# Attention into two gated layers on one core: loads held 16 units back, other transfer prices in the plan, words scaled on GpSimd

## The chip, the cores and the metric

The kernel runs on one core of one Trainium2 chip. The metric is the device time of one execution in microseconds (us); lower is better. TensorE (PE) multiplies matrices, VectorE (DVE), ScalarE (ACT) and GpSimd (POOL) do element work, and SyncE (SP) issues nearly all transfers, in the order of its own queue.

## What is computed

```python
def _attn_ref(q, k, v, g_q, g_k):        # q, k, v: (4, 12, 448, 64)
    ...
    q_n, k_n = (rmsnorm(q, g_q), rmsnorm(k, g_k))
    scale = 1.0 / np.sqrt(q.shape[-1])
    scores = scale * np.matmul(q_n, k_n.transpose(0, 1, 3, 2))
    ...                                  # softmax over the last axis gives attn
    return np.matmul(attn, v).astype(np.float32)

def _moe_ref(x, w_in, w_out):            # w_in (768, 2048), w_out (2048, 768)
    h = x @ w_in
    relu6 = np.clip(h + 3.0, 0.0, 6.0)
    g = h * relu6 / 6.0
    return (g @ w_out).astype(np.float32)

def _moe2_ref(x, w_in, w_out):
    h = x @ w_in
    r = np.maximum(h, 0.0)
    g = r * r
    return (g @ w_out).astype(np.float32)

    # reference: x is the attention output as (1792, 768)
    x = _moe_ref(x=x, **moe_kwargs)
    return _moe2_ref(x=x, **moe2_kwargs)
```

Attention comes first, for 4 batches of 12 heads; its result passes through two layers, each a product into 2048 columns, a gate, and a product back to 768.

## The kernel before, in words

**Numbers in two halves.** Products run in f16. Each float32 operand is split into a high and a low f16 half, and three of the four products of halves are added. The weights arrive as 64-bit words, and `convert` makes them into halves, one unit at a time: `load` (DMA into a tile `wr`), `sign` on DVE into a tile `wf`, `dx` (a multiplication of the high words by 2^-112, on ACT or DVE), `d1` (a byte of the low words, on ACT), `join` on DVE, a maximum, a scale for the family of units, and the split into `ws` (`hi` and `lo`). The halves are used at once and stored (`spill`); later units with the same weights load them from there (`again`).

**Units.** `UNITS` lists 272 units of products in the order in which PE does them: for each layer m and batch b, 16 "in" units (18 products each) and 18 "out" units (18 or 15 products), the last 6 of them behind the next batch's "in" units. There are 4608 products in all (L1014), each 128x128 by 128x448. Batch b of the first layer needs the attention of batch b: its "in" units begin at product 0, 480, 1056 and 1632. Units 0 to 27 and 44 to 49 convert the first layer's weights, units 130 to 163 and 180 to 185 the second layer's.

**Attention.** A step (b, p) takes two heads. `norms` loads q and k (`qk`), squares and sums them, takes the inverse root on GpSimd (L448 to L453), scales, splits, and transposes by DMA into `T` (L513); two more transfers make `W`, with the halves swapped. PE makes scores (`ps_s`, L696), DVE the row maximum, ACT the exponential. In the 11 steps named in `ACROSS`, PE transposes the exponentials (L666) and multiplies in float32 (L773). In the other 13 the probabilities are split (`p`) and transposed by DMA into `pt` (L741), and PE multiplies there (`ps_a`, L792).

**What sets the order.** `Plan.order` is a list scheduler that runs when the program is built. Each task has a key, the engines on which it can run with a guessed time, tasks it depends on, and buffers. `STEPS`, `SCALE` and `VMAX` give the keys of attention's tasks in units of the products; `LOOK` and `LOOK0` say how many units ahead weights are loaded and converted. A transfer (`xfer`) is put one behind the other on a single line. The scheduler only writes down the order of each engine and which engine does a task that may run on two; on the chip every engine takes its list in order and waits where data or a buffer is missing.

Of the kernel before, what the change touches and what calls it, by code (L numbers as in the profile page):

```python
# [37 lines left out]
def units():  # L38
# [19 lines left out]
STEPS = (  # L58
    (-85.2638, -84.5299, -76.4585, -66.4326, -62.0971, -61.7424),
    (-14.9266, -4.9125, 0.9188, 14.2707, 1.5272, 9.9697),  # L60
    (28.6516, 33.3075, 36.1555, 43.5753, 49.5311, 53.688),
    (67.1629, 67.9195, 73.2971, 102.3362, 73.5949, 89.3515),
)
SCALE = (0.4278, 0.4, 0.6456, 0.4916)
VMAX = (-67.3424, 17.8405, 50.7595, 55)

SHORT = {1, 2}
LOOK = (4.0538, 5.2083)
LOOK0 = (8.2895, 6.1085, 2.0783)
GROUP = (1, 2, 2, 2)  # L70
# [34 lines left out]
class Plan:  # L105
# [168 lines left out]
def tile_kernel(ctx: ExitStack, tc: tile.TileContext, qk, v, vn, g, ident, w1i, w1o, w2i, w2o, out):  # L274
    nc = tc.nc
# [112 lines left out]
    def norms(j, p, k0, sc):  # L388
# [127 lines left out]
        if fast:  # L516
# [30 lines left out]
            t_l1 = task(km + .04, [("DVE", dve2(448), lambda: los(1))], [t_h1], [vq, vsrc])  # L547
            t_t0 = task(km + .1, [("SP", 600, lambda: trs(0))], [t_l0], [vsrc, vT], xfer=800)
            t_w = task(km + .12, [("SP", 600, tr_rev)], [t_lr, t_hr], [vrev, vW], xfer=800)
            t_tr = task(km + .11, [("SP", 600, lambda: trs(1))], [t_l1], [vsrc, vT], xfer=800)  # L550
            t_trs = [t_t0, t_tr]
            first.append(t_w)
        else:
# [3 lines left out]
            t_lo = task(k0 - 14.7 * sc, [("DVE", dve2(896), lo)], [t_hi], [vq, vsrc])  # L557
            t_trs = [task(k0 - 14.6 * sc, [("SP", 1200, tr)], [t_lo], [vsrc, vT], xfer=1570)]
        prep[b, p] = vT, t_trs, vW, t_w


    def attention(j, p, k0, sc):
# [157 lines left out]
        for r in range(0 if across else NT):  # L720
# [16 lines left out]
            for x in rows[r]:  # L737

                def ptr(r=r, vp=vp, x=x):
                    h, a, z, at, col = x  # L740
                    nc.sync.dma_start_transpose(  # L741
                        out=tl(vpt[h], [P, NV, n], F16)[:, :, col:col + z - a],
                        in_=tl(vp)[at:at + z - a, r % 2].rearrange("p a t -> p (a t)"),
                    )

                t_pt[x[0]].append(task(kk + 2.2 * sc, [("SP", 650, ptr)], [t_pl], [vp, vpt[x[0]]], xfer=(x[2] - x[1]) * 6))

# [118 lines left out]
    def convert(m, i0, ns):  # L866
# [5 lines left out]
        for x, (i, n) in enumerate(zip(ids, ns)):  # L872
# [117 lines left out]
    def unit(b, m, i, n):  # L990
# [17 lines left out]
        for a, z in cuts:  # L1008
# [257 lines left out]
```

## Time and profile before

| | |
|---|---|
| median of 3 runs | 1203.03 us (1201.07 to 1203.38) |
| the profiled execution | 1209.35 us, of which the profile's span is 1207.6 us |
| TensorE | 1123.3 us busy, 93% of the span, mean granted clock 0.977 |
| VectorE | 719.0 us, 60% |
| ScalarE | 703.9 us, 58% |
| GpSimd | 104.2 us, 9% |
| DMA | 231.18 MB moved, mean 191 GB/s |

Shares are means over the whole span. Up to about 607 us attention, conversion and products run side by side; behind that there are products, gates and the second layer's conversion alone. The mean granted clock is in parts of the full TensorE clock of 2.4 GHz; its other level is half of it.

### The profile page before, as it was taken

The numbers are of one execution on the slowest core, as the hardware profiler recorded it, in microseconds if no ns is written. First come the engines' busy times: TensorE is split into PE (matmuls) and PEld (weight loads), VectorE is DVE, ScalarE is ACT, GpSimd is POOL, SyncE is SP. The second block draws the span as 40 slices with busy tenths as digits, with TensorE's granted clock in tenths as the row PEclk, the third lists the DMA queues.
The fourth block names the chain that finished last, engine by engine and source line by source line (L and its number), as shares of the span: only waits on it lengthen the run. The fifth ranks groups of instructions, "written<-read, shape, count | busy, mean of one in ns | idle before, by whom it ended". The sixth has DMA issues, their size and how long they took to land.

```text
span 1207.6 us, 17036 instructions
## 1 busy us (share of the span) xinstructions
PE 1123.3 (93%) x6070; PEld 583.7 (48%) x6070; DVE 719.0 (60%) x1653; ACT 703.9 (58%) x1375; POOL 104.2 (9%) x142
## 2 busy tenths in 40 slices
PE   1889999799899989989999999999999999999998
PEld 0455555355444444434445545454455555555554
DVE  6989999989799967887813527878126000200300
ACT  2889899998778767755711417977356033213400
POOL 3511211101111211120000000000000000000000
PEclk9989999799999989998999999999999999999999
DMA  9755567679999899998643366869736444453351
GB/s 251 216 166 156 187 200 251 200 180 304 224 282 272 220 220 259 211 205 175 168 125 118 109 197 213 289 209 317 284 101 204 160 141 130 124 168 103 105 159 54
DMA packets 214743, 231.18 MB, mean 191 GB/s; under 512 B 137873, under 2 KB 174865, under 8 KB 214657
## 3 DMA queue, kind: packets, MB, share of 16 engines
q1 hardware_dynamic: 214592, 229.95, 66.6%
q8 instruction: 48, 0.79, 0.3%
q14 instruction: 39, 0.31, 0.1%
q0 software_dynamic: 64, 0.13, 0.1%
HBM read 156.47 MB, written 36.18 MB: 160 GB/s over the span
## 4 chain that ended last, share of the span: by engine, by line
PE 61%; DVE 14%; DMA 12%; ACT 9%; issue 2%; SPq 1%; POOL 1%; ACTq 0%; DVEq 0%
PE m L1014 49%; PE ps_s L696 3%; PE ps_a L792 3%; PE ps_s L666 2%; PE ps_a L773 2%; DVE nm L703 2%; DMA pt_0B<-p 2%; DMA qk<-in_qk_dram 1%; DMA wr<-in_w2o_dram 1%; ACT wf L898 1%; PE ps_r L759 1%; DMA ws<-spill 1%; ACT wr L889 1%; DVE p L733 1%; DVE ws L942 1%
## 5 line engine op out<-in xcount | busy, mean ns | idle before, releaser
L1014 PEld LDWEIGHTS <-ws 128*128 128x128 f16 x4608 | 446.1, 98 | 427.7 <-issue 18.5
L1014 PE MATMUL m<-g,ws 128*128 128x448 f16 x2304 | 459.5, 354 | 5.2 <-DVE g L1111 2.6
L1014 PE MATMUL m<-x,ws 128*128 128x448 f16 x1152 | 234.8, 353 | 1.3 <-DMA ws<-spill 0.9
L1014 PE MATMUL m<-yk,ws 128*128 128x448 f16 x1152 | 221.4, 353 | 0.6 <-DMA ws<-spill 0.6
L656 ACT ACTIVATE e<-ps_s,nm,esc 128x448 f32<-128x448 f32 x168 | 121.8, 726 | 22.4 <-DVE nm L713 22.0
L703 DVE TENSOR_REDUCE nm<-ps_s 128x1 f32<-128x448 f32 x168 | 102.6, 615 | 9.7 <-PE ps_s L696 9.3
L1045 ACT ACTIVATE t<-m,inv 128x448 f32<-128x448 f32 x64 | 39.5, 622 | 99.2 <-PE m L1014 99.1
L1194 ACT ACTIVATE o<-m,ov 128x448 f32<-128x448 f32 x24 | 14.5, 630 | 137.1 <-PE m L1014 137.1
L1043 ACT ACTIVATE t<-m,half,six 128x448 f32<-128x448 f32 x64 | 46.0, 721 | 58.9 <-PE m L1014 58.8
L901 DVE TENSOR_SCALAR wf<-wr 128x768 int32<-128x768 int32 (+1 forms) x68 | 35.8, 531 | 55.9 <-PE m L1014 50.5
L898 ACT ACTIVATE wf<-wr 128x768 uint8<-128x768 uint32 (+1 forms) x68 | 68.6, 1014 | 0.0
L696 PE MATMUL ps_s<-T,W 128*128 128x448 f16 (+1 forms) x192 | 63.0, 373 | 5.4 <-DMA W<-W_0r 2.8
L905 DVE SCALAR_TENSOR_TENSOR wf<-wr,wf 128x768 int32<-128x768 int32 (+1 forms) x68 | 61.4, 905 | 9.8 <-ACT wf L898 9.4
L942 DVE SCALAR_TENSOR_TENSOR ws<-wf,w_s,ws 128x768 f16<-128x768 f32 (+1 forms) x68 | 65.1, 963 | 3.1 <-ACT ws L935 2.5
L696 PE MATMUL ps_s<-T 128*128 128x448 f16 (+1 forms) x192 | 63.7, 379 | 0.2 <-DVE xr L779 0.2
L666 PE MATMUL ps_s<-eye,e 128*112 128x128 f32 x308 | 51.2, 302 | 12.1 <-ACT e L656 11.9
L1049 DVE SCALAR_TENSOR_TENSOR gr<-t,m 128x448 f32<-128x448 f32 x64 | 39.4, 616 | 38.7 <-ACT t L1043 38.3
L1052 DVE SCALAR_TENSOR_TENSOR gr<-t 128x448 f32<-128x448 f32 x8 | 5.0, 621 | 94.7 <-ACT t L1045 94.6
L733 DVE SCALAR_TENSOR_TENSOR p<-e,su,p 128x448 f16<-128x448 f32 x91 | 59.7, 678 | 1.8 <-ACT p L727 1.3
L889 ACT ACTIVATE wr<-wr 128x768 f32<-128x768 f32 (+1 forms) x60 | 52.2, 870 | 13.7 <-DVE wf L901 13.7
L337 DVE TENSOR_REDUCE g_s<-gm 128x1 f32<-128x16 f32 x4 | 0.7, 164 | 95.8 <-ACT gr L1055 95.6
L727 ACT ACTIVATE p<-e,su 128x448 f16<-128x448 f32 x78 | 49.4, 659 | 10.0 <-DVE su L642 4.7
(202 smaller groups left out, 1305.8 us busy)
## 6 DMA issues: line engine op xcount, KB each, us to landing
ws<-spill SPq DMA_DIRECT2D x132, 384.0 KB, 3.5
ws<-spill SPq DMA_DIRECT2D x72, 320.0 KB, 3.5
spill<-ws SPq DMA_DIRECT2D x44, 384.0 KB, 4.0
wr<-in_w1i_dram SPq DMA_DIRECT2D x16, 768.0 KB, 5.3
wr<-in_w2i_dram SPq DMA_DIRECT2D x16, 768.0 KB, 6.0
qk<-in_qk_dram SPq DMA_DIRECT2D x23, 448.0 KB, 4.7
wr<-in_w1o_dram SPq DMA_DIRECT2D x12, 640.0 KB, 4.9
spill<-ws SPq DMA_DIRECT2D x24, 320.0 KB, 4.8
```

The lines of the kernel that those rows point to most:

```text
L656: nc.scalar.activation(tl(ve)[:, r % 2], tl(vps)[:, 0:S], AF.Exp, bias=sums["nm"][:, r:r + 1], scale=esc, accum_out=sums["su"][:, r:r + 1])
L666: nc.tensor.transpose(o[:, c], tl(ve)[:, r % 2, c * VR:(c + 1) * VR], eye)
L696: nc.tensor.matmul(ps[at:at + z - a, 0:S], q_[:, a:z], ks[:, h * S:(h + 1) * S], start=(i == 0), stop=(i == 1))
L703: nc.vector.tensor_reduce(sums["nm"][:, r:r + 1], tl(vps)[:, 0:S], axis=AX.X, op=ALU.max, negate=True)
L727: nc.scalar.activation(tl(vp)[:, r % 2, 0], tl(ve)[:, r % 2], AF.Copy, scale=sums["su"][:, r:r + 1])
L733: nc.vector.scalar_tensor_tensor(tl(vp)[:, r % 2, 1], tl(ve)[:, r % 2], sums["su"][:, r:r + 1], tl(vp)[:, r % 2, 0], op0=ALU.mult, op1=ALU ...
L889: nc.scalar.activation(x_, x_, AF.Copy, scale=2.0 ** -112)
L898: nc.scalar.activation(low, l_.bitcast(U32), AF.Copy, scale=2.0 ** -29 * (1 - 2.0 ** -9), bias=-0.49)
L905: nc.vector.scalar_tensor_tensor(w, words()[1], 3, w, op0=ALU.logical_shift_left, op1=ALU.bitwise_or)
L942: nc.vector.scalar_tensor_tensor(tl(vws)[:, 1, 0:nf].rearrange("p k c -> p (k c)"), tl(vwf)[:, 0:nw], up, hi, op0=ALU.mult, op1=ALU.subtract)
L1014: nc.tensor.matmul(tl(vph)[:, 0:S], w[:, wa, k], tl(rhs[k])[:, xa], start=(first_ and k == 0 and c == 0), stop=(last and k == nf - 1 and c ...
L1043: nc.scalar.activation(tl(vt), tl(vph)[:, 0:S], AF.Relu, bias=half, scale=six[:, row:row + 1])
```

## The change

Five kinds of edit, all in the tables and tasks of the plan, and one new way to run a task.

1. `STEPS`, `SCALE`, `VMAX`, `LOOK`, `LOOK0` get other numbers, which changes the keys and with them the order on every engine.
2. The guessed line time of a transfer is raised: 1570 to 3600 for the transposing of q and k, 800 to 1800 for its quick form, 6 to 13 per column for probabilities.
3. A load of weights' words for unit n + 16 becomes a successor of unit n's first product task (`LAG`). This dependence is in the plan alone: it moves the load in SP's order.
4. `dx` may run on GpSimd, as two multiplications by 2^-56 in one instruction; the plan gives it 200 + 4/3 ns a word.
5. One limit in `GUESTS` goes from 16 to 15. All the tags it counts share class "A", which has 13 buffers.

```diff
 STEPS = (
-    (-85.2638, -84.5299, -76.4585, -66.4326, -62.0971, -61.7424),
...
+    (-204.52957392941647, -218.06331192668318, -196.15344590088333, -194.49856021390312, -188.4550482489744, -188.10503386389664),
...
-SCALE = (0.4278, 0.4, 0.6456, 0.4916)
-VMAX = (-67.3424, 17.8405, 50.7595, 55)
+SCALE = (0.17829075341655345, 0.49480955532248644, 0.6115384885049036, 0.1729590704995054)
+VMAX = (-33.350052814676175, 26.349410516927087, 21.48448662340024, 32.12299918329385)
-LOOK = (4.0538, 5.2083)
-LOOK0 = (8.2895, 6.1085, 2.0783)
+LOOK = (3.8790651137382435, 1.1102033712882977)
+LOOK0 = (7.419866410034254, 6.101668435784244, 1.4427606568871552)
+LAG = 16
-    (("qk", "sq", "src", "T", "v", "v16", "e", "p16"), 16),
+    (("qk", "sq", "src", "T", "v", "v16", "e", "p16"), 15),
...
-            t_trs = [task(k0 - 14.6 * sc, [("SP", 1200, tr)], [t_lo], [vsrc, vT], xfer=1570)]
+            t_trs = [task(k0 - 14.6 * sc, [("SP", 1200, tr)], [t_lo], [vsrc, vT], xfer=3600)]
...
-                t_pt[x[0]].append(task(kk + 2.2 * sc, [("SP", 650, ptr)], [t_pl], [vp, vpt[x[0]]], xfer=(x[2] - x[1]) * 6))
+                t_pt[x[0]].append(task(kk + 2.2 * sc, [("SP", 650, ptr)], [t_pl], [vp, vpt[x[0]]], xfer=(x[2] - x[1]) * 13))
...
+            def dx_p(words=words):
+                x_ = words()[1].bitcast(F32)
+                nc.gpsimd.tensor_scalar(x_, x_, 2.0 ** -56, 2.0 ** -56, op0=ALU.mult, op1=ALU.mult)
...
+            opened[n] = t_l
-            t_x = task(kc + .05, [("ACT", act(nw), dx_a), ("DVE", dve1(nw), dx_v)], [t_2], [vwr])
+            t_x = task(kc + .05, [("Pool", 200 + 4 * nw // 3, dx_p), ("ACT", act(nw), dx_a), ("DVE", dve1(nw), dx_v)], [t_2], [vwr])
...
+            if not a and n + LAG in opened:
+                late = opened[n + LAG]
+            else:
+                late = None
             t = task(n + (.1 if a else 0), [("PE", 3 * (z - a) * 190, mm)], [t_w, *dep[a:z], *prev], [vws, vph, *rhs[a:z]])
             last_mm[0] = t
+            if late:
+                t.after.append(late)
+                late.left += 1
```

How the change moves the order is shown at three places. Line numbers differ by a few between the two files; the number behind a name's prefix is the unit (`m_90`, `ws_91`, `wr_130`) or the step (`ps_a_3_5` is batch 3, step 5).

**The last step of attention.** PE's queue before, where the last `ps_a` of attention begins; `m_90` with `ws_91` is a product of unit 91, in the "out" units of batch 2.

```order
L1014 MATMUL m_90_6479<-g_2_0_9_6282,ws_91_6487 128x448
L1014 LDWEIGHTS ws_91_6487
L1014 MATMUL m_90_6479<-g_2_0_9_6282,ws_91_6487 128x448
L792 LDWEIGHTS v16_3_5_6325
L792 MATMUL ps_a_3_5_6560<-pt_3_5A_6461,v16_3_5_6325 64x448
```

The same place on PE now; `m_97` is a product of unit 97, in the "in" units of batch 3.

```order
L1022 MATMUL m_97_6589<-x_3_0_5281,ws_97_6500 128x448
L1022 LDWEIGHTS ws_97_6500
L1022 MATMUL m_97_6589<-x_3_0_5281,ws_97_6500 128x448
L793 LDWEIGHTS v16_3_5_6379
L793 MATMUL ps_a_3_5_6593<-pt_3_5A_6442,v16_3_5_6379 64x448
```

1566 of the 4608 products stood ahead of it before, and 1644 stand ahead of it now. SP's queue before, where the same step's queries and keys are transposed (`ws_84` and the like are reloads of converted weights for those units).

```order
L958 DMA ws_84_6039<-spill_78 128x1536
L513 DMA_TRANSPOSE T_3_5_6045<-src_3_5_6012 128x14x128
L741 DMA_TRANSPOSE pt_3_3B_5995<-p16_3_3_4_6020 128x7x128
L958 DMA ws_85_6090<-spill_78 128x2x640
L584 DMA W_3_5_6106<-T_3_5_6045 64x896
```

The same place on SP now.

```order
L964 DMA ws_87_5999<-spill_78 128x1536
L514 DMA_TRANSPOSE T_3_5_6013<-src_3_5_5953 128x14x128
L964 DMA ws_88_6055<-spill_78 128x2x640
L964 DMA ws_89_6086<-spill_78 128x2x640
L585 DMA W_3_5_6094<-T_3_5_6013 64x896
```

The transposing moved from behind unit 84's reload to behind unit 87's, 48 products (18 + 15 + 15), and the product that needs the step's end moved by 78.

**The first loads of the second layer's words.** SP's queue before, among the transfers of attention's batch 2.

```order
L398 DMA qk_2_4_3651<-in_qk_dram 128x896
L958 DMA ws_38_3666<-spill_78 128x1536
L881 DMA wr_130_3674<-in_w2i_dram 128x1536
L958 DMA ws_39_3697<-spill_78 128x1536
L584 DMA W_2_3_3708<-T_2_3_3638 64x896
L585 DMA W_2_3_3708<-T_2_3_3638 64x896
L881 DMA wr_131_3724<-in_w2i_dram 128x1536
L741 DMA_TRANSPOSE pt_2_1B_3562<-p16_2_1_4_3738 128x7x128
```

The place of the same loads on SP now, behind all of attention.

```order
L964 DMA ws_120_7145<-spill_78 128x2x640
L882 DMA wr_130_7164<-in_w2i_dram 128x1536
L964 DMA ws_121_7173<-spill_78 128x1536
L882 DMA wr_131_7175<-in_w2i_dram 128x1536
L882 DMA wr_132_7183<-in_w2i_dram 128x1536
```

Eight such loads (units 130 to 137) stood ahead of the end of attention before; none does now.

**Conversion of unit 12.** ACT's queue before: L889 is `dx`, L898 `d1`.

```order
L809 ACTIVATE x_1_1_1800<-xr_1_1_1789 128x448
L889 ACTIVATE wr_12_1703<-wr_12_1703 128x768
L898 ACTIVATE wf_12_1765<-wr_12_1703 128x768
L656 ACTIVATE e_1_2_2_1824,su_1_2_1680<-ps_s_1_2_2_1700,nm_1_2_1679,esc_73 128x448
L656 ACTIVATE e_1_2_2_1824,su_1_2_1680<-ps_s_1_2_3_1774,nm_1_2_1679,esc_73 128x448
```

ACT's queue there now; L903 is `d1`.

```order
L903 ACTIVATE wf_11_1718<-wr_11_1525 128x768
L903 ACTIVATE wf_12_1737<-wr_12_1596 128x768
L674 COPY pt_1_1B_1677<-ps_s_1_1_6_1664 112x4x128
L657 ACTIVATE e_1_2_0_1761,su_1_2_1702<-ps_s_1_2_0_1690,nm_1_2_1701,esc_73 128x448
L657 ACTIVATE e_1_2_0_1761,su_1_2_1702<-ps_s_1_2_1_1713,nm_1_2_1701,esc_73 128x448
```

GpSimd's queue there now, with `dx` of units 11 and 12 ahead of the next step's inverse root.

```order
L898 TENSOR_SCALAR wr_11_1525<-wr_11_1525 128x768
L898 TENSOR_SCALAR wr_12_1596<-wr_12_1596 128x768
L449 TENSOR_SCALAR ss_1_4_1906<-ss_1_4_1906 128x14
L450 TENSOR_TENSOR rs_1_4_1926<-ss_1_4_1906,mhalf_74 128x14
L451 TENSOR_TENSOR rt_1_4_1927<-rs_1_4_1926 128x14
```

`dx` left ACT's queue: of the 68, GpSimd has 63 now (30 of them ahead of attention's end), ACT 1 and DVE 4; before, ACT had 60 and DVE 8.

## Rows read from the trace of the kernel before

**Rows 1.** The page: span, engines' busy time, and the chain's shares by engine.

```profile
span 1207.6 us, 17036 instructions
PE 1123.3 (93%) x6070; PEld 583.7 (48%) x6070; DVE 719.0 (60%) x1653; ACT 703.9 (58%) x1375; POOL 104.2 (9%) x142
PE 61%; DVE 14%; DMA 12%; ACT 9%; issue 2%; SPq 1%; POOL 1%; ACTq 0%; DVEq 0%
```

**Rows 2.** Five stretches: length, busy us of each engine, granted clock, DMA share, GB/s.

```profile
33.00:93.00 60.00, 52.61 (x279) 31.36 (x280) 53.81 (x126) 52.24 (x114) 17.11 (x23) 0.89 0.67 185
93.00:212.00 119.00, 116.82 (x715) 65.95 (x712) 114.40 (x262) 113.44 (x223) 21.43 (x30) 1.00 0.65 200
212.00:247.00 35.00, 26.76 (x126) 14.38 (x127) 31.89 (x77) 32.38 (x65) 5.36 (x6) 0.76 0.60 179
247.00:607.00 360.00, 329.69 (x1819) 166.27 (x1819) 301.06 (x699) 262.18 (x527) 48.17 (x66) 0.97 0.93 229
607.00:1207.00 600.00, 591.20 (x3120) 303.63 (x3114) 195.35 (x437) 235.45 (x438) 0.00 (x0) 1.00 0.51 166
```

**Rows 3.** Waits of PE, 247 to 607 us: in total, times, longest.

```profile
PE ps_a L792 <- DMA pt_4B<-p: 8.4, 2, 6.0
PE ps_a L792 <- issue: 5.7, 2, 3.2
PE ps_a L792 <- DMA pt_0B<-p: 3.3, 2, 3.1
```

**Rows 4.** Timeline of PE: the last step's `ps_a` (start, us, idle before it).

```profile
606.65 0.35 PE L792 MATMUL ps_a<-pt_5B,v 128*64 128x448 f16 x1 [2.49 <-issue]
```

**Rows 5.** The chain that ended last, 915 to 1207 us: two long pieces.

```profile
916.64 106.80 PE m L1014 x564
1024.98 107.93 PE m L1014 x570
```

**Rows 6.** The chain by line, 33 to 247 and then 247 to 607 us.

```profile
by line: PE m L1014 14.3%; PE ps_s L666 9.7%; PE ps_a L773 8.2%; PE ps_s L696 8.1%; PE ps_r L759 6.0%; DVE nm L703 4.8%; ACT e L656 4.4%; ACT wf L898 3.4%; ACT wr L912 3.0%; ACT wr L889 2.8%; issue 2.6%; DMA wr<-in_w1i_dram 2.4%; ACT ws L93
by line: PE m L1014 26.8%; PE ps_a L792 8.0%; DMA pt_0B<-p 5.8%; PE ps_s L696 4.8%; DMA qk<-in_qk_dram 4.6%; issue 3.8%; DVE p L733 3.5%; DVE nm L703 3.4%; DVE g L1111 2.6%; SPq L741 2.5%; DMA pt_2B<-p 2.4%; DMA pt_5B<-p 2.4%; DMA pt_4B<-p 
```

**Rows 7.** Loads of words on SP, 300 to 607 us: times of issue min/median/max ns.

```profile
L881 SPq DMA_DIRECT2D wr<-in_w2i_dram x8: 328/452/1527, 340.9 to 486.0; - x8
```

**Rows 8.** Conversion and attention's last steps by form: count | busy us, mean ns.

```profile
L905 DVE SCALAR_TENSOR_TENSOR wf<-wr,wf 128x768 int32<-128x768 int32 x44 | 41.8, 951 | 5.6 <-ACT wf L898 5.2
L901 DVE TENSOR_SCALAR wf<-wr 128x768 int32<-128x768 int32 x44 | 24.1, 554 | 6.1 <-PE m L1014 2.1 <-DMA wr<-in_w2i_dram 2.0 <-DMA wr<-in_w2o_dram 1.2
L898 ACT ACTIVATE wf<-wr 128x768 uint8<-128x768 uint32 x44 | 46.8, 1067 | 0.0
L889 ACT ACTIVATE wr<-wr 128x768 f32<-128x768 f32 x38 | 34.7, 914 | 11.1 <-DVE wf L901 11.1
L809 ACT ACTIVATE x<-ps_a 128x448 f16<-128x448 f32 x13 | 6.9, 539 | 21.0 <-PE ps_a L792 21.0
L818 DVE SCALAR_TENSOR_TENSOR x<-ps_a,x 128x448 f16<-128x448 f32 x13 | 7.9, 618 | 19.3 <-ACT x L809 19.3
```

**Rows 9.** `dx` on DVE, up to 607 us: min/median/max ns.

```profile
L893 DVE TENSOR_SCALAR wr<-wr x3: 555/556/558, 63.4 to 149.2; 128x768 f32<-128x768 f32 x3
```

**Rows 10.** Timeline of DVE and GpSimd beside each other, 406 to 414 us.

```profile
406.49 3.64 DVE L1173 SCALAR_TENSOR_TENSOR y<-yr,y_s,y 128x448 f16<-128x448 f32 x6
406.64 3.59 POOL L448 TENSOR_SCALAR ss<-ss 128x14 f32<-128x14 f32 x1 [35.24 <-DVE ss L419]
410.31 2.58 POOL L449 TENSOR_TENSOR rs<-ss,mhalf 128x14 f32<-128x14 f32 x1
410.82 0.86 DVE L619 SCALAR_TENSOR_TENSOR v<-v,v_s,v 128x256 f16<-128x256 f32 x2
413.56 0.21 POOL L452 TENSOR_SCALAR rt<-rt 128x14 f32<-128x14 f32 x1
```

**Rows 11.** By form: the mean of that DVE instruction over the whole span.

```profile
L619 DVE SCALAR_TENSOR_TENSOR v<-v,v_s,v 128x256 f16<-128x256 f32 x26 | 11.4, 477 | 0.1
```

More of the change, by code (lines that the diff above doesn't have):

```diff
@@ L58 @@
 STEPS = (
-    (-85.2638, -84.5299, -76.4585, -66.4326, -62.0971, -61.7424),
-    (-14.9266, -4.9125, 0.9188, 14.2707, 1.5272, 9.9697),
-    (28.6516, 33.3075, 36.1555, 43.5753, 49.5311, 53.688),
-    (67.1629, 67.9195, 73.2971, 102.3362, 73.5949, 89.3515),
-)
-SCALE = (0.4278, 0.4, 0.6456, 0.4916)
-VMAX = (-67.3424, 17.8405, 50.7595, 55)
+    (-204.52957392941647, -218.06331192668318, -196.15344590088333, -194.49856021390312, -188.4550482489744, -188.10503386389664),
+    (-54.94523213706141, -51.120116320052794, -40.04124726459441, 14.59012713343561, -28.86315002428371, 6.40996083307427),
+    (29.136992352402334, 39.058582380350174, 35.95175679635861, 45.03139474291142, 41.134610109639794, 52.14402846271607),
+    (66.93461228183692, 70.84500965107601, 73.3617039469757, 129.48682583028543, 76.91247771902272, 89.59611422135544),
+)
+SCALE = (0.17829075341655345, 0.49480955532248644, 0.6115384885049036, 0.1729590704995054)
+VMAX = (-33.350052814676175, 26.349410516927087, 21.48448662340024, 32.12299918329385)
 SHORT = {1, 2}
-LOOK = (4.0538, 5.2083)
-LOOK0 = (8.2895, 6.1085, 2.0783)
+LOOK = (3.8790651137382435, 1.1102033712882977)
+LOOK0 = (7.419866410034254, 6.101668435784244, 1.4427606568871552)
 GROUP = (1, 2, 2, 2)
@@ L547, in norms @@
             t_l1 = task(km + .04, [("DVE", dve2(448), lambda: los(1))], [t_h1], [vq, vsrc])
-            t_t0 = task(km + .1, [("SP", 600, lambda: trs(0))], [t_l0], [vsrc, vT], xfer=800)
-            t_w = task(km + .12, [("SP", 600, tr_rev)], [t_lr, t_hr], [vrev, vW], xfer=800)
-            t_tr = task(km + .11, [("SP", 600, lambda: trs(1))], [t_l1], [vsrc, vT], xfer=800)
+            t_t0 = task(km + .1, [("SP", 600, lambda: trs(0))], [t_l0], [vsrc, vT], xfer=1800)
+            t_w = task(km + .12, [("SP", 600, tr_rev)], [t_lr, t_hr], [vrev, vW], xfer=1800)
+            t_tr = task(km + .11, [("SP", 600, lambda: trs(1))], [t_l1], [vsrc, vT], xfer=1800)
             t_trs = [t_t0, t_tr]
@@ L963, in tile_kernel @@
     fresh = {}
+    opened = {}
     gval, gdone, yval, ydone, pm = {}, {}, {}, {}, {}
```

## The prediction

> **What bounds the kernel now.** The page comes first: PE is busy for 93% of the span and holds 61% of the chain that ended last; DVE has 14% of it, DMA 12%, ACT 9% [rows 1]. The work of PE doesn't change: 4608 products before and after, and the same steps of attention. So time can be won only where PE waits or runs at the lower of its two clocks (1.2 in place of 2.4 GHz), and the stretches say where that is [rows 2]. Behind 607 us PE is busy for 591.2 of 600 us. Ahead of it, from 33 to 607 us, it is idle for 60.0 − 52.6 = 7.4, 2.2, 8.2 and 360.0 − 329.7 = 30.3 us, 48.1 in all. What the clock took, as length times the part not granted, is 60 × 0.11 + 35 × 0.24 + 360 × 0.03 = 25.8 us. So 74 us are there to be won in 574; the first 33 us are a chain through the first step's transfers, whose order hardly changes, and I leave them.
>
> The biggest waits between 247 and 607 us are those for transposed probabilities, `pt` [rows 3]. The last of them, 2.49 us, ends at 606.65 us, where attention's last `ps_a` begins [rows 4]. In this stretch the DMA engines are 0.93 busy and DVE 301.1 of 360 us [rows 2], and under half of the chain is PE's (26.8% products, 8.0% and 4.8% attention); the rest goes through transfers of `pt` and `qk`, DVE and SP [rows 6]. Attention's pipeline, not PE, sets the pace there; PE fills in with products as far as the order lets it.
>
> That gives a sum to work with: time = the end of attention + what is left for PE then. Attention ended at 606.65 with 1566 products done, and the remaining 3042 with all their waits took 1207.6 − 606.65 = 600.95 us. A product that runs behind others takes 106.80 / 564 = 107.93 / 570 = 0.1894 us [rows 5].
>
> **The change, part by part.**
>
> *The new keys and transfer times.* The last `ps_a` stands behind 1644 products now, 78 more. If attention ends when it did, PE has 78 × 0.1894 = 14.8 us less to do afterwards: **−14.8**. PE can do them earlier, since 74 us were lost ahead of that point. The hidden condition is that attention isn't held up by those products in turn. SP's queue couples the two, since a reload waits for a buffer that PE must free, and the transposing of the last step moved by 48 products. That is less than 78, so the distance from transposing to use grows by 30 products, 5.7 us, more than the last wait of 2.49 us [rows 4]. Bounds: 0 if the end of attention moves by as much as the products do, and −74 + 15 = −59 more if every wait from 33 us on goes.
>
> The end of batch 3's attention now stands inside that batch's own first units, so PE has nearly nothing else when it comes; behind the last `ps_a` a rounding on ACT and the low half on DVE follow before the next product, 0.54 + 0.62 [rows 8]. Before, unit 91's products covered them: **+1.2**.
>
> *Eight loads of words leave attention's stretch.* Between 340.9 and 486.0 us SP issued eight loads of the second layer's words [rows 7], each 128 × 1536 words of 4 bytes; they stand behind attention now. That is 6.3 MB of the 360 × 229 GB/s = 82.4 MB which the stretch moved [rows 2], 7.6%. Transfers hold at least 5.8 + 4.6 + 2.4 + 2.4 = 15.2% of the chain there, 54.7 us [rows 6]; 7.6% of that is **−4.2**. Bounds: 0 if the loads sat in gaps between transposes, −27 (7.6% of 360) if the DMA engines are the limit all the while. Where these loads go, from about product 2050 on, DVE and ACT are busy for 195 and 235 of 600 us [rows 2], and the first product that needs them is number 2208, 156 products or 29.5 us on: nothing.
>
> *Five fewer conversions ahead of attention's end.* DVE has 34 of `sign` and `join` there, and had 39: 5 × (0.55 + 0.95) = 7.5 us [rows 8], of which DVE's share of the chain counts. That share is at most 0.14 × 1207.6 = 169 of 574 us, 29% [rows 1]: **−2.2**.
>
> *`dx` on GpSimd, the ACT side.* A `dx` on ACT takes 0.91 us and stands ahead of `d1` on the same engine, 1.07 us [rows 8]. `join` needs both. Between 33 and 247 us `dx` holds 2.8% of the chain, 214 × 0.028 = 6.0 us [rows 6]. On GpSimd it runs beside `d1`: **−6.0** if it takes no longer than `d1`; what is late next is `d1` itself. Behind 247 us `dx` isn't among the lines of the chain that the view names, so nothing there.
>
> *`dx` on GpSimd, its own price.* No GpSimd instruction of this size is in the trace. The smallest like it is L452, 14 elements in 0.21 us; on DVE the same `dx` takes 0.56 us [rows 9], and that is the lower bound. The upper one is L448: 3.59 us, because it started 0.15 us behind six DVE instructions that each read two SBUF tensors, and ended 0.10 us behind the last of them [rows 10]. GpSimd got nothing between the six. The other way round, two such instructions took 0.86 us inside the 2.58 us of L449, no more than their mean of 0.48 each [rows 10, 11]. So a short GpSimd instruction doesn't slow DVE, and DVE can starve GpSimd; what 768 elements do to DVE, no row shows. I take half of DVE's own 0.56 us for each of the 30 scalings ahead of attention's end, 0.28 × 30 = 8.4 us of DVE, 29% of it on the chain: **+2.4**. Bounds: 0, and 30 × (3.59 − 1.07) = 76 if DVE idles at each `join` for a starved `dx`.
>
> On this the Trainium skill (SBUF — State Buffer, Who interferes with whom) speaks against the change: VectorE and GpSimd share a pair of ports, and a VectorE instruction with two SBUF inputs against a GpSimd instruction that reads SBUF is an exclusive lock, in which the later one stands still until the first is done. L448 agrees with that in one direction; L619 inside L449 doesn't show the other. The Trainium skill (GPSIMD Engine Reference, 3.1 Elementwise — side-by-side cycle accounting) gives 769 ns for 512 elements of a simple loop, which makes an estimate of 1.15 us for 768; with the lock costing DVE all of it, 30 × 1.15 × 0.29 = +10.0 would stand in place of +2.4.
>
> *Without effect.* The limit of 15 in `GUESTS` can't bind with 13 buffers. `LOOK`'s second number leaves the loads of `yk` at the same units. Both at nothing, since the order shows it.
>
> **Sum.** −14.8 + 1.2 − 4.2 − 2.2 − 6.0 + 2.4 = −23.6. The profiled execution took 1209.35 us, so 1185.8 for one like it. The median before is 6.3 us below the profiled execution, 1203.0; 1203.0 − 23.6 = **1179 us**. A measurement of this kernel tells about 0.2%, 2.4 us, from no change.
>
> **Rivals.** (a) *Only the products move.* The pace of attention is that of its transfers (0.93 busy), the relief on ACT and the loads sit in gaps, and the end stays at 606.65: 1203.0 − 14.8 = 1188. For it speaks that DVE's work ahead of that point shrinks by a few us only. 25%.
>
> (b) *Most stalls go.* Distances from transposing to use grow at most steps, and with better prices in the plan fewer queues stand blocked; then half of the 59 us left goes as well: 1203.0 − 14.8 − 30 = 1158. Against it: DVE, 301 of 360 us busy, would have to run without gaps (the same DVE work in 330 us is 0.91), and it does that only between 93 and 212 us (114.4 of 119). 13%.
>
> (c) *Attention stays tied to the products*, through SP's reloads, and ends 78 products later too: 1203. Against it, the 30 products gained in distance. 12%.
>
> (d) *GpSimd starves*, the one that ends slower. `join` waits in DVE's queue for a `dx` that DVE itself held up, and behind it on DVE stand row maxima and the halves of probabilities that PE waits for. At half of the upper bound, 1.3 us each on the path, 30 × 1.3 = 39 against the −26.0 of the other terms: 1203 + 13 = 1216. It decides from 26.0 / 30 = 0.87 us on the path for each scaling. For it speaks the row with 3.59 us, against it the L619 row, and that other DVE work stands between `sign` and `join` in the order. 14%. The lock that the Trainium skill describes (SBUF — State Buffer, Who interferes with whom) would do this, and in both directions.
>
> **Chances.** Forecast 36% (its own range is 1172, with the loads at some 40% of their bound, to 1186, with `dx` on ACT at 0), (a) 25%, (b) 13%, (c) 12%, (d) 14%. The range from 1157 to 1207 leaves out (d) and about half of (b). Faster by over 0.2%: the forecast, (a), (b) and a quarter of (c), 77%; within 0.2%: most of (c), 7%; slower: (d) and what is left, 16%.
>
> **What would show it.** Right: the last `ps_a` begins between 590 and 605 us; the waits of L792's successor for `pt` shrink below 10 us in all; no loads of the second layer's words in DMA ahead of it; `dx` on GpSimd near 1 us; the `dx` line gone from the chain between 33 and 247 us. Wrong: DVE's `join` idle for GpSimd by more than 20 us in all, DVE's two-input instructions longer than in [rows 8], or PE waiting for the last `x` at product 1644 by more than 10 us, which would say that attention's pipeline didn't get faster. A start later than 33 us would also upset the sum.

## The result, and the profile after

The changed kernel takes **1184.87 us** (median of 4 runs, 1183.87 to 1188.25), the kernel before 1203.2 (4 runs): ratio **0.9844**, interval 0.9803 to 0.9886, faster by 1.6%. Forecast were 1179 us and a range of 1157 to 1207. Profiled execution against profiled execution it is 1183.87 − 1209.35 = −25.5 us, where the sum had −23.6; the difference of the medians is −18.3, because the profiled execution before lay 6.2 us above the 1203.2 and the one after lies 1.0 below its own.

The page of the changed kernel: span, engines and the chain by engine, to be read against [rows 1].

```profile
span 1182.1 us, 17164 instructions
PE 1109.6 (94%) x6070; PEld 573.3 (48%) x6070; DVE 726.4 (61%) x1644; ACT 670.0 (57%) x1324; POOL 167.0 (14%) x205
PE 68%; DVE 20%; DMA 4%; issue 3%; ACT 3%; POOL 1%; SPq 1%; DVEq 0%; ACTq 0%; POOLq 0%
```

DMA's share of the chain fell from 12 to 4% and ACT's from 9 to 3%; DVE's rose from 14 to 20%. The stretches of the changed kernel, in the columns of [rows 2], with attention's end at 593 in place of 607:

```profile
33.00:93.00 60.00, 48.76 (x290) 28.20 (x290) 58.20 (x134) 53.26 (x117) 22.85 (x28) 1.00 0.75 207
93.00:212.00 119.00, 113.73 (x684) 62.74 (x681) 113.19 (x254) 100.25 (x200) 37.46 (x42) 0.99 0.64 194
212.00:247.00 35.00, 30.20 (x140) 15.51 (x138) 31.42 (x75) 31.89 (x65) 7.10 (x10) 0.79 0.58 177
247.00:593.00 346.00, 336.46 (x1907) 169.10 (x1906) 296.23 (x676) 245.95 (x504) 53.45 (x75) 0.99 0.97 230
593.00:1182.00 589.00, 575.40 (x3045) 295.72 (x3039) 203.34 (x455) 232.02 (x433) 35.49 (x33) 1.00 0.52 173
```

PE's idle time in the fourth stretch is 346.0 − 336.5 = 9.5 us; it was 30.3, so 20.8 us came from there. It wasn't free: ahead of 247 us PE is idle for 11.2 + 5.3 + 4.8 = 21.3 us (17.8 before), and behind attention's end for 13.6 (8.8 before). The clock took 119 × 0.01 + 35 × 0.21 + 346 × 0.01 = 12.0 us, after 25.8, so the clock gave back 13.8 us. Together that is −20.8 − 13.8 + 3.5 + 4.8 = −26.3, near the −25.5 (the view rounds the clock to 0.01, which is 3.6 us in the fourth stretch before).

PE's biggest waits between 247 and 593 us (answering to [rows 3]), then behind 593 us:

```profile
PE m L1022 <- DVE ws L948: 2.5, 1, 2.5
PE ps_a L793 <- DMA pt_5B<-p: 2.1, 1, 2.1
PE ps_s L697 <- ACT e L657: 1.8, 1, 1.8
```

```profile
PE w_p L341 <- DVE w_s L338: 5.1, 4, 1.9
PE w_p L350 <- DVE w_s L347: 1.5, 2, 0.8
```

Of the waits for `pt` one of 2.1 us is left. PE's timeline where attention's last product group begins ([rows 4] before):

```profile
592.25 0.38 PE L793 MATMUL ps_a<-pt_5B,v 128*64 128x448 f16 x1
```

It begins at 592.25 us, 14.4 earlier, though 78 more products stand ahead of it, and what follows takes 1182.1 − 592.25 = 589.85 us, 11.1 less than before. The chain by line, 33 to 247 and then 247 to 593 us ([rows 6] before; the view cuts these lines at their end):

```profile
by line: DVE nm L704 11.9%; PE ps_a L774 7.3%; DMA qk<-in_qk_dram 6.9%; issue 6.1%; PE ps_s L667 5.9%; PE m L1022 5.0%; DVE wf L910 4.8%; DVE ws L948 4.7%; PE ps_r L760 4.3%; DVE qk L484 3.2%; ACT e L657 2.7%; DVE nm L714 2.6%; DVE wf L906 
by line: PE m L1022 54.6%; PE ps_s L697 7.6%; PE ps_a L793 7.1%; DVE nm L704 2.8%; DVE p L734 2.8%; issue 2.6%; DVE g L1126 2.2%; DMA pt_5B<-p 2.2%; DVE ws L948 1.4%; DVE wf L910 1.3%; SPq L742 1.2%; DVE qk L484 1.0%; DVE v L620 1.0%; PE ps
```

Between 247 us and attention's end products hold 54.6% of the chain in place of 26.8%: PE sets the pace there now. Ahead of that, `dx` and `d1` on ACT no longer stand in the part of the line that is shown, and the row maximum (`nm`, L704) and `join` (L910) on DVE have come up. The tiles of conversion (count: min/median/max ns, first and last start):

```profile
L898 POOL TENSOR_SCALAR wr<-wr x63: 772/910/1727, 48.7 to 882.5; 128x768 f32<-128x768 f32 x41, 128x640 f32<-128x640 f32 x22
L910 DVE SCALAR_TENSOR_TENSOR wf<-wr,wf x68: 799/944/1529, 53.1 to 883.4; 128x768 int32<-128x768 int32 x44, 128x640 int32<-128x640 int32 x24
L882 SPq DMA_DIRECT2D wr<-in_w2i_dram x16: 327/377/957, 653.6 to 735.2; - x16
```

`dx` on GpSimd takes 0.91 us in the median, and the second layer's first words are loaded from 653.6 us on.

### The profile page after: what moved, and what is told of

It reads as the page before. It is cut to its first block, busy times and chain, and to the rows that moved or that the text cites. A ratio compares the mean times of both kernels' runs of the same rounds, so it can differ in the third digit from the quotient of the medians.

```text
span 1182.1 us, 17164 instructions
## 1 busy us (share of the span) xinstructions
PE 1109.6 (94%) x6070; PEld 573.3 (48%) x6070; DVE 726.4 (61%) x1644; ACT 670.0 (57%) x1324; POOL 167.0 (14%) x205
## 4 chain that ended last, share of the span: by engine, by line
PE 68%; DVE 20%; DMA 4%; issue 3%; ACT 3%; POOL 1%; SPq 1%; DVEq 0%; ACTq 0%; POOLq 0%
PE m L1022 59%; DVE nm L704 3%; PE ps_s L697 3%; PE ps_a L793 2%; DVE ws L948 2%; DVE wf L910 2%; PE ps_a L774 2%; DVE g L1126 1%; DMA qk<-in_qk_dram 1%; PE ps_s L667 1%; DVE qk L484 1%; DVE wf L906 1%; PE ps_r L760 1%; DMA vx<-in_vn_dram 1%; DVE p L734 1%
## 5 line engine op out<-in xcount | busy, mean ns | idle before, releaser
L898 POOL TENSOR_SCALAR wr<-wr 128x768 f32<-128x768 f32 (+1 forms) x63 | 65.7, 1045 | 455.3 <-DVE wf L906 306.8
L704 DVE TENSOR_REDUCE nm<-ps_s 128x1 f32<-128x448 f32 x168 | 102.2, 614 | 6.4 <-PE ps_s L697 6.1
L903 ACT ACTIVATE wf<-wr 128x768 uint8<-128x768 uint32 (+1 forms) x68 | 69.4, 1026 | 34.2 <-DVE wf L906 28.9
L910 DVE SCALAR_TENSOR_TENSOR wf<-wr,wf 128x768 int32<-128x768 int32 (+1 forms) x68 | 63.2, 930 | 12.8 <-ACT wf L903 7.8
L667 PE MATMUL ps_s<-eye,e 128*112 128x128 f32 x308 | 48.5, 292 | 13.1 <-ACT e L657 12.8
L917 ACT ACTIVATE wr<-wf 128x768 f32<-128x768 f32 (+1 forms) x62 | 50.1, 809 | 17.1 <-DVE wf L910 16.7
```

The lines of the kernel that those rows point to most:

```text
L667: nc.tensor.transpose(o[:, c], tl(ve)[:, r % 2, c * VR:(c + 1) * VR], eye)
L704: nc.vector.tensor_reduce(sums["nm"][:, r:r + 1], tl(vps)[:, 0:S], axis=AX.X, op=ALU.max, negate=True)
L898: nc.gpsimd.tensor_scalar(x_, x_, 2.0 ** -56, 2.0 ** -56, op0=ALU.mult, op1=ALU.mult)
L903: nc.scalar.activation(low, l_.bitcast(U32), AF.Copy, scale=2.0 ** -29 * (1 - 2.0 ** -9), bias=-0.49)
L910: nc.vector.scalar_tensor_tensor(w, words()[1], 3, w, op0=ALU.logical_shift_left, op1=ALU.bitwise_or)
L917: nc.scalar.activation(tl(vwr).bitcast(F32)[:, 0:nw], tl(vwf)[:, 0:nw], AF.Abs, accum_out=mx[:, x:x + 1])
```

## The experiments

The theory to be tested: two gains, the distance between a step's scores and its `ps_a` (products that stand between them on PE), which takes away the waits for `pt`, and `dx` leaving ACT. Rivals: that the loads moved out of attention's stretch do it, or the keys, or that GpSimd's price on DVE eats the second gain. The four kernels of each group ran on one chip together with the kernel before, which took 1206.8, 1205.3 and 1206.4 us in the three groups; so ratios are compared.

### First group: the changed kernel with one part undone

**`dx` back on ACT**, in the places that the plan gave to GpSimd; the orders of PE, DVE and SP stay.

```diff
-                nc.gpsimd.tensor_scalar(x_, x_, 2.0 ** -56, 2.0 ** -56, op0=ALU.mult, op1=ALU.mult)
+                nc.scalar.activation(x_, x_, AF.Copy, scale=2.0 ** -112)
```

> The changed kernel with every order kept, but the 63 scalings that stand in GpSimd's queue are issued to ACT instead, at the place in ACT's queue where the plan wrote them down. My account: between 33 and 247 us the scaling comes back in front of the byte conversion, which costs about 6 us there, and the 2.4 us for GpSimd's use of shared ports come back; so about 1188 to 1190 against about 1185 for the changed kernel. Rival, that the scaling on GpSimd is the main source of the gain: 1195 or more. Rival, that GpSimd costs DVE more than it frees on ACT: below 1183.

Measured: 1197.27 us, ratio 0.9923 (0.9896 to 0.995), 0.79% or 9.5 us behind the changed kernel by the ratios (the two intervals don't overlap). That is more than the 3 to 5 us expected and nearer to the first rival's time. Attention's last step begins at 596.89 us, 4.6 later, and the rest takes 595.5, 5.7 longer. DVE's waits at `join` in this kernel, then in the changed one:

```profile
DVE wf L910 <- ACT wr L898: 16.0, 13, 1.9
DVE wf L910 <- ACT wf L903: 15.8, 15, 3.5
```

```profile
DVE wf L910 <- ACT wf L903: 7.8, 9, 2.6
DVE wf L910 <- POOL wr L898: 4.9, 5, 1.1
```

31.8 us of waiting against 12.7. DVE is busy for 715.7 us here and 726.4 there with the same list: 63 scalings on GpSimd cost DVE 10.7 us, 0.17 each. So the GpSimd way is worth 9.5 us net in this order, more than half of it behind attention's end, where the sum had nothing. (A plan made for ACT would have placed `dx` otherwise; that wasn't tried.)

**`dx` twice on GpSimd**: a second instruction that multiplies by 1, which changes no value.

```diff
+                nc.gpsimd.tensor_scalar(x_, x_, 1.0, 1.0, op0=ALU.mult, op1=ALU.mult)
```

> The changed kernel with a second GpSimd instruction behind each scaling that multiplies the same words by 1, so the GpSimd price of a scaling doubles (to about 1.8 to 2 us) and nothing else changes. My account (hidden beside the byte conversion of 1.07 us and other DVE work between the two DVE steps): at most 8 us more, since only the part beyond 1.07 us can be waited for, 1185 to 1193. Rival, that each scaling lies on the path or locks DVE for its length: 30 x 0.9 = 27 us ahead of the end of attention, so 1200 or more.

Measured: 1206.89 us, ratio 1.0 (0.998 to 1.0021); against the changed kernel +19 us by the ratios, 0.30 per scaling. At most 8 us were expected; the rival's 1200 us or more came. `join` waits for GpSimd for longer, and `join` itself grew from 962 to 1050 ns for 768 words (this kernel's DVE waits, then its instructions by form):

```profile
DVE wf L911 <- POOL wr L899: 25.1, 27, 2.1
```

```profile
L911 DVE SCALAR_TENSOR_TENSOR wf<-wr,wf 128x768 int32<-128x768 int32 x44 | 46.2, 1050 | 15.6 <-POOL wr L899 15.2 <-ACT wf L904 0.4
```

A scaling of twice the length would have cost the whole gain: the way over GpSimd is close to the path. That `join` waits for GpSimd, one half of rival (d), is seen here at twice the length; that DVE itself held those scalings up, the other half, this kernel doesn't show.

**No lag for the loads**: the dependence finds no unit.

```diff
-LAG = 16
+LAG = 1000
```

> The changed kernel without the 16-unit dependence, everything else as changed; the plan then puts eight or more of the second layer's loads back among attention's transfers, and the last step of attention behind 1500 products. My account: it loses 144 products of 0.189 us that PE did ahead of the end of attention, 27 us, less what attention ends earlier with fewer products to wait for, so about 1195 to 1205. Rival, that the dependence does little and the transfer prices do the work: within 3 us of the changed kernel, 1182 to 1188.

Measured: 1215.04 us, ratio 1.0065 (1.0043 to 1.0086), slower than before; the expectation was missed. The plan is made anew, so more than the loads moves. Attention ends about as in the changed kernel, at 593.23 us, but only 1500 products stand ahead of it, and PE waits for weights instead of `pt` (its waits, 247 to 625 us):

```profile
PE m L1022 <- DMA ws<-spill: 15.2, 7, 7.5
PE m L1022 <- ACT ws L941: 5.4, 1, 5.4
```

Eight loads of the second layer's words (323.8 to 461.5 us) and 39 conversions lie ahead of attention's end here. It comes 1 us later than in the changed kernel, but with 144 fewer products ahead of it, so this doesn't say what the loads cost.

**The second layer's loads 28 units back**, twelve units earlier than in the changed kernel's plan for them.

```diff
-            if not a and n + LAG in opened:
-                late = opened[n + LAG]
+            if not a and n + (LAG if n < 100 else 28) in opened:
+                late = opened[n + (LAG if n < 100 else 28)]
```

> The changed kernel with the second layer's loads held back 28 units in place of 16; the first layer's stay at 16, and all of attention keeps its place among the products. PE idles 10.1 us behind the end of attention in the changed kernel where the waits name DVE steps of conversion or the weights' scales, against 3.1 us before. If that is because the loads begin too late, those waits fall to 3 to 5 us and the time by 4 to 6, to about 1180. If it is because conversion and gates together fill ACT and DVE between 700 and 830 us, the time stays within 2 us.

Measured: 1187.28 us, ratio 0.984 (0.9811 to 0.9869): no difference from the changed kernel. The loads begin at 608.3 us, 45 us earlier, and PE's idle time behind attention doesn't shrink for it (16.5 us here, 13.6 there): loads that begin too late aren't its cause.

### Second group: the kernel before with one part added

**`dx` on GpSimd in the order of before** (the inverse of the first edit).

> The kernel before with every order kept, but the 60 scalings that stood in ACT's queue are issued to GpSimd. In the changed kernel, giving them back to ACT cost about 10 us and the two DVE steps' wait rose from 13 to 32 us. If that holds whatever the order is, this gains 6 to 11 us: ratio 0.991 to 0.995. Rival, that the scaling on GpSimd pays only in an order laid out for it, with ACT's time used by other work: within 0.3% of before, or slower, because GpSimd's queue has the inverse roots of the next step behind it.

Measured: 1212.0 us, ratio 1.0059 (1.0038 to 1.0081): slower, where a gain was expected and the rival had no gain or a loss. DVE's busy time went from 719.0 to 732.0 us, 13.0 / 60 = 0.22 a scaling, while `join` waited for 8.4 us in all (9.4 before): little was to be freed there, and the price was left.

**The lag alone**: the rules of edit 3, old keys and prices.

```diff
+LAG = 16
...
+            if late:
+                t.after.append(late)
+                late.left += 1
```

> The kernel before with the 16-unit dependence alone, the plan made again. The last step of attention stands behind 1650 products (before 1566, changed 1644), and no load of the second layer stands ahead of it. My account, by which time = end of attention + what is left: 84 x 0.189 = 16 us less to do behind it and 4 us for the loads; but the last four steps stand within 33 products of each other (1617 to 1650), so PE waits for them there. I expect a gain of 5 to 15 us, ratio 0.988 to 0.996. Rival, that the dependence without the dearer transfers does nothing: within 0.3%.

Measured: 1227.26 us, ratio 1.0178 (1.0147 to 1.0209), the slowest of all; a gain was expected. The last step has 1650 products ahead of it, and begins 15.1 us later than before, behind a wait for its `pt` (PE's timeline, then its waits, 247 to 625 us):

```profile
621.71 0.55 PE L793 MATMUL ps_a<-pt_5B,v 128*64 128x448 f16 x1 [4.44 <-DMA pt_5B<-p]
```

```profile
PE ps_a L793 <- DMA pt_4B<-p: 9.6, 3, 3.7
PE ps_a L793 <- DMA pt_1B<-p: 4.7, 2, 4.5
```

The second layer's loads are behind attention here (from 685.0 us), and the time is longer all the same.

**The transfer prices alone.**

```diff
-...[t_lo], [vsrc, vT], xfer=1570)]
+...[t_lo], [vsrc, vT], xfer=3600)]
-... xfer=(x[2] - x[1]) * 6))
+... xfer=(x[2] - x[1]) * 13))
```

> The kernel before with the dearer transfers in the plan alone. The last step of attention stands behind 1632 products, 66 more than before, with the second layer's loads still among attention's transfers. By my account 66 x 0.189 = 12 us less is left behind the end, and the distance from scores to use is longer at most steps: a gain of 5 to 12 us. Rival, that the tables of keys were made for the old prices and the new ones alone spoil them: slower by more than 0.3%.

Measured: 1190.41 us, ratio 0.987 (0.9845 to 0.9895). That is 14.9 us, more than the 5 to 12 expected, and the interval overlaps the whole change's: three numbers of the plan give about as much.

**The keys alone** (`STEPS`, `SCALE`, `VMAX`, `LOOK`, `LOOK0` of the change).

> The kernel before with the new tables of keys alone (STEPS, SCALE, VMAX, LOOK, LOOK0). The last step of attention stands behind 1629 products. Without the 16-unit dependence the changed kernel was slower than before, so by my account keys alone give nothing or a loss: ratio 0.998 to 1.012. Rival, that the keys are the change and the rest is dressing: 0.984 to 0.990.

Measured: 1214.48 us, ratio 1.0089 (1.0057 to 1.0121): slower, as expected. Attention ends 9.5 us later, at 616.16.

### Third group: which price, and with GpSimd

**Prices half way** (1300, 2600, 9.5 a column), **the price of q and k alone**, **the price of probabilities alone**, each in the kernel before. The edit of the last:

```diff
-... xfer=(x[2] - x[1]) * 6))
+... xfer=(x[2] - x[1]) * 13))
```

> The kernel before with transfer prices about half way between the old and the new ones (2600 for the transposing of q and k, 1300 for its quick form, 9.5 per column), nothing else changed. If the prices work because they make the plan's distances match the chip's, half the step gives part of the gain: ratio 0.988 to 0.996 (the full step gave 0.987). If the full step's gain is the luck of one order among many, this one can fall anywhere, as the two other part changes did (1.009 and 1.018).

> The kernel before with the new price for the transposing of q and k alone (3600, quick form 1800). Its four last steps of attention stand behind 1383, 1608, 1638 and 1650 products, as crowded as in the kernel with the 16-unit dependence alone, which was slower by 1.8%. I expect little: 0.995 to 1.010. Rival, that this price is the one that counts, because T is what everything behind it waits for: 0.985 to 0.992.

> The kernel before with the new price for the transposing of probabilities alone (13 per column). There are eight of these transfers in a step against one of q and k, and the waits of PE before were for them; the last steps stand behind 1521, 1569 and 1629 products. I expect most of the gain of both prices: 0.986 to 0.993. Rival, that both are needed: 0.995 or more.

Measured: 1198.83 us, ratio 0.9932 (0.9905 to 0.9958), for half way; 1203.26, 0.9973 (0.9954 to 0.9991), for q and k; **1184.59, 0.9814 (0.9788 to 0.9841)**, for probabilities. One number does as much as the whole change; its interval overlaps the whole change's, so no order between the two is claimed. Half way and q and k came within what was expected of them; the price of probabilities gave more. Its stretches around attention, and its waits on PE between 247 and 625 us:

```profile
247.00:607.00 360.00, 342.13 (x1937) 170.97 (x1933) 308.01 (x715) 252.62 (x505) 46.75 (x66) 0.99 0.99 235
607.00:1182.00 575.00, 565.76 (x2987) 291.11 (x2985) 190.55 (x430) 232.34 (x432) 0.00 (x0) 1.00 0.52 168
```

```profile
PE m L1014 <- DMA ws<-spill: 4.5, 6, 1.6
...
PE ps_a L792 <- DMA pt_5B<-p: 3.8, 1, 3.8
```

In the same 247 to 607 us PE is busy for 342.1 instead of 329.7 us at a clock of 0.99 instead of 0.97 ([rows 2]), and one wait for `pt`, of 3.8 us, is left. Eight loads of the second layer's words still lie in that stretch. Half way and q and k keep waits at attention's last step (PE's timeline, half way first):

```profile
614.62 0.55 PE L792 MATMUL ps_a<-pt_5B,v 128*64 128x448 f16 x1 [4.14 <-DMA pt_5B<-p]
```

```profile
610.86 0.53 PE L792 MATMUL ps_a<-pt_5B,v 128*64 128x448 f16 x1 [4.76 <-DMA pt_5B<-p]
```

**Both prices and the GpSimd way**, planned anew with old keys and no lag.

> The kernel before with both new transfer prices and with GpSimd as a way for the scaling, the plan made again; old keys, no 16-unit dependence. By itself in the old order the scaling on GpSimd cost 0.6%, and in the changed order it gave 0.8 to 0.9%. If it pays once the plan knows of it, this is faster than the prices alone: 0.978 to 0.985, the fastest of all. If it needs the new keys as well: 0.985 to 0.995.

Measured: 1200.17 us, ratio 0.9946 (0.9928 to 0.9965), 0.8% slower than the prices without it; the fastest of all was expected. The whole plan differs, and attention ends 2.6 us later than with the prices alone, so this isn't GpSimd's price on DVE by itself.

## Why the prediction was right, and where its terms were not

The frame of the prediction's sum is what happened: attention's last step begins earlier with more products done, and less is left behind it. What it summed inside the frame is not: `dx`, put at −3.6, was worth some 10, and the waits for `pt` and the clock, which gave most of the time ahead of the last step, had no term.

The table has all kernels by the prediction's sum: products ahead of the last step's `ps_a`; when its first product with `pt_5B` begins; what follows; that less 0.1894 us for each product still to do; PE's waits for `pt` in `ps_a` between 247 and 625 us; and the products between a step's last scores and its `ps_a` (batches 2 and 3, mean / least).

Times are those of the one profiled execution of each kernel (half way's was 5.7 us slower than its median). A dash: not read; PE's order there is that of the changed kernel or of before. The waits include those that the view puts down to `issue` (5.7 us before, 0.6 with q and k's price): the last of them, 2.49 us before 606.65 ([rows 4]), ends where a transfer of `pt_5B` issued at 603.7 and 2.9 to 3.2 us on its way lands.

| kernel | ratio | products | begin | rest | rest − products | waits for `pt` | distance |
|---|---|---|---|---|---|---|---|
| before | 1 | 1566 | 606.65 | 600.95 | 24.8 | 23.6 | 70 / 30 |
| changed | 0.9844 | 1644 | 592.25 | 589.85 | 28.5 | 2.1 | 100 / 60 |
| changed, `dx` on ACT | 0.9923 | 1644 | 596.89 | 595.5 | 34.1 | – | – |
| changed, `dx` twice | 1.0 | 1644 | 602.28 | 603.7 | 42.3 | – | – |
| changed, no lag | 1.0065 | 1500 | 593.23 | 617.7 | 29.0 | 0 | 96 / 63 |
| changed, 28 units | 0.984 | 1644 | 593.55 | 592.9 | 31.5 | – | – |
| before, `dx` on GpSimd | 1.0059 | 1566 | 609.08 | 601.6 | 25.4 | – | – |
| before, lag | 1.0178 | 1650 | 621.71 | 606.8 | 46.6 | 28.8 | 78 / 39 |
| before, keys | 1.0089 | 1629 | 616.16 | 595.5 | 31.3 | 10.1 | 83 / 57 |
| before, prices | 0.987 | 1632 | 600.70 | 588.2 | 24.5 | 1.0 | 89 / 60 |
| before, half way | 0.9932 | 1650 | 614.62 | 588.1 | 27.9 | 12.5 | 107 / 60 |
| before, q and k | 0.9973 | 1650 | 610.86 | 588.4 | 28.2 | 16.5 | 104 / 66 |
| before, probabilities | 0.9814 | 1629 | 595.18 | 587.5 | 23.3 | 3.8 | 110 / 84 |
| before, prices and GpSimd | 0.9946 | 1617 | 603.32 | 593.8 | 27.3 | 0 | 104 / 51 |

**The frame held.** What follows attention is 0.1894 us a product plus 23 to 34 us in all but two kernels; those two have 42.3 (`dx` twice) and 46.6 (lag alone). The scatter of 11 us is more than half of the change's gain, so a small difference between two kernels can't be read off the products alone.

**The −14.8 for 78 products** came as −11.1 together with the +1.2: 3.7 us more were lost behind the last step than before, not 1.2. But the term doesn't mark this change. Keys, lag and prices, alone, each put 63 to 84 more products ahead of the last `ps_a`, and of these kernels two are slower than before (keys, lag) and one hardly faster (q and k's price). Its condition, "if attention ends when it did", decides: alone, the lag, the keys, q and k's price and the half-way prices moved the end back by 4 to 15 us. This is the outcome of rival (c), that attention stays tied to the products, and these kernels went its way in part; the changed kernel didn't.

**The end of attention** came 14.4 us earlier, where the terms for it add up to −4.2 − 2.2 − 6.0 + 2.4 = −10.0. The size is near, the make-up is not, so the nearness is luck in part:

- *Eight loads, −4.2, and five conversions, −2.2*: no run shows either. Without the lag, and with the price of probabilities alone, loads and all 39 conversions lie ahead of the end, which comes at 593.23 and 595.18; with the lag alone they are gone, and it comes at 621.71. An early end doesn't need them gone, and their being gone doesn't bring one. These plans differ in all else too, so what the two terms are worth isn't measured; nothing speaks against their lower bound of 0.
- *`dx` on GpSimd, −6.0 + 2.4 = −3.6*: measured ahead of the end, 4.6, and 5.7 behind it, where the prediction put nothing. Its price on DVE is 0.17 to 0.22 us a scaling, estimated 0.28. The gain was there where `join` had waited for ACT (31.8 us with `dx` on ACT, 12.7 now); in the old order, where it waited for 9.4, the same edit lost 0.6%.
- *The waits for `pt`*: the prediction read them first ([rows 3]) and then gave them no term; they sat in rival (b). They fell from 23.6 to 2.1 us. The plan with 6 ns a column counted these transfers too short: for 128 columns 650 + 768 + 1476 ns, 2.9 us from issue to end, where the medians before are 3.0 to 4.9 us by tile. With 13 (3.8 us) their products stand farther behind the scores (from 70 to 110 in the mean for that price alone, the least from 30 to 84). That this distance is the whole cause isn't shown: half-way prices and q and k's price have 107 and 104 and still wait for 12.5 and 16.5 us. In each of these two, 7.4 us of the waits are at the last step (3.3 + 4.1 and 2.6 + 4.8), whose own distance is 84; the kernel with both prices has 63 there and no wait. What does sort the orders of PE is how close the last steps stand: in the four whose end came later by 4 us or more the last three steps' `ps_a` begin within 33 (lag), 42 (half way, q and k) and 63 products (keys), in the others within 108 to 222. That fits attention being held up by its own steps crowding each other, but no run changes that alone; what SP's order adds stays open.
- *The clock*: it stood among the 74 us to be won and got no term. It gave back some 13.8 of the 29.2 us (14.4 + 14.8) that were won ahead of the last step.

**Moved loads, "nothing"**: PE is idle for 13.6 us behind attention against 8.8, and 6.6 of them are waits for `w_s`, the weights' scales, on DVE (2.6 before). The moved loads aren't shown to be the cause. Loads 28 units back changed nothing; and without the lag, where eight loads and five conversions are back ahead of attention's end, PE is idle for 617.67 − 602.58 = 15.1 us behind it, with these waits behind 593 us:

```profile
PE w_p L341 <- DVE w_s L338: 4.9, 5, 1.9
PE w_p L350 <- DVE w_s L347: 3.1, 3, 1.7
```

PE's idle time there is 16.2 us with the new keys alone, 22.4 with the lag alone and 13.8 with prices and the GpSimd way, but 9.9 with the price of probabilities and 10.5 with both prices. So several parts of the change can bring it, and the cause stays open.

**The first 33 us** weren't wholly neutral: PE's first scores with `W` begin 1.8 us later (30.38 against 28.57), and from 33 to 93 us PE is idle for 11.2 us, before 7.4.

**The rivals.** (a) falls, since the end moved. (d) falls at one instruction: `join` waits for GpSimd for 4.9 us in all, and the point from which it decides, 0.87 us a scaling, isn't reached; doubling the instruction brought 0.30 a scaling and 1.6%. One of the prediction's signs of being wrong came weakly: `join` takes 962 and 870 ns for 768 and 640 words, after 951 and 820. (b) came in part: 21 us of idle time went from attention's stretch, and some 8 came back elsewhere.

**From the sum to the median.** For the two profiled executions the sum is right to 2 us (−23.6 against −25.5); for the medians it is 5.3 us too large (−18.3). Its terms were read from a profiled execution that was 6.2 us slower than its kernel's median, and the sum was then taken from the median; that is most of the distance from 1179 to 1184.9.

What stays open: the changed kernel with the old prices and the changed kernel planned without the GpSimd way weren't run, so how much each part gives inside the whole is known for the lag and, in a fixed order, for GpSimd alone. Each new plan is also one order among many: q and k's price gains 0.3% by itself and loses 0.6% beside the price of probabilities, so some of any one number here can be the luck of its order.

## What to carry to other kernels

Where a plan made ahead of time sets every engine's order, look first for a resource that it prices below what the trace shows and on which the busiest engine waits: one number for such transfers brought as much as the whole change, while new keys or a new dependence alone lost 0.9 and 1.8%. A low price alone isn't enough: the transposing of q and k was counted as 4.2 us (1200 + 1570 + 1476 ns) and took 5.4 in the median, and raising its price gave 0.3%. Compute a reordering as "when does the last step begin" plus "what is left then", and treat a later place of that step as a gain only once its own inputs are seen to come early. Work moved to a free engine paid where somebody waited for the engine that it left; in the other order only its price remained.

## What the runs showed of the hardware

**DVE and GpSimd stop each other, both ways.** The changed kernel's timeline around 143 and 679 us (start, us, idle before):

```profile
143.41 0.94 POOL L898 TENSOR_SCALAR wr<-wr 128x768 f32<-128x768 f32 x1 [3.27 <-ACT wf L903]
143.71 1.46 DVE L910 SCALAR_TENSOR_TENSOR wf<-wr,wf 128x768 int32<-128x768 int32 x1
...
678.94 0.95 DVE L910 SCALAR_TENSOR_TENSOR wf<-wr,wf 128x768 int32<-128x768 int32 x1
679.17 1.53 POOL L898 TENSOR_SCALAR wr<-wr 128x768 f32<-128x768 f32 x1 [0.73 <-ACT wf L903]
```

`join` started 0.30 us behind a scaling and took 1.46 us, 0.51 more than its 0.95; the scaling had 0.64 us left. A scaling that started 0.23 us behind a `join` took 1.53, 0.62 more than its 0.91. Whichever came second stood still for most of what the first had left. Three more scalings that start 0.22 to 0.23 us behind a `join` take 1.36 to 1.51 us. This is what the Trainium skill (SBUF — State Buffer, Who interferes with whom) says of a VectorE instruction with two SBUF inputs against a GpSimd one that reads SBUF; these rows show the direction that [rows 10] left open. The estimate of 1.15 us for the scaling from the Trainium skill (GPSIMD Engine Reference, 3.1 Elementwise — side-by-side cycle accounting) was above the 0.91 of the median; with the standstills the mean of the 41 scalings of 768 words is 1.11.

**The granted clock didn't follow PE's idle time alone.** Two stretches of before, and then of the changed kernel:

```profile
53.00:63.00 10.00, 7.96 (x38) 3.96 (x38) 9.65 (x25) 9.37 (x25) 5.45 (x6) 0.77 0.51 182
73.00:83.00 10.00, 8.28 (x42) 5.88 (x44) 8.26 (x34) 6.92 (x15) 3.74 (x6) 0.66 0.55 185
```

```profile
53.00:63.00 10.00, 8.85 (x55) 4.55 (x53) 9.90 (x26) 9.86 (x24) 3.70 (x6) 1.00 0.56 154
73.00:83.00 10.00, 8.01 (x55) 4.42 (x53) 9.90 (x30) 9.64 (x22) 5.13 (x4) 1.00 0.49 145
```

From 73 to 83 us PE is busy for 8.01 us at 1.00 after and for 8.28 at 0.66 before, that is, part of the time at the lower of its two levels; over 33 to 93 us that gave back 60 × 0.11 = 6.6 us, more than the 3.8 us of idle time which the stretch gained. Over the same 33 to 93 us the kernel with the new keys alone has 0.97, the changed one with `dx` on ACT 0.94, and the one before with `dx` on GpSimd 0.89. So most of the difference comes with the keys; what in them makes it stays open.
